# A fused three-block kernel: attention values share the transposes' PSUM bank, dense work gets a third bank, first-batch v tiles are released a third of a step later

## The chip, the cores and the metric

The kernel runs on one core of one Trainium2 chip, in one launch. The metric is the device time of that core in microseconds (us), as a median over runs. One execution was also recorded with the hardware profiler; its trace is what is read below.

## What is computed

Three blocks follow each other. `x` has 4 batches of 576 positions and 512 channels.

```python
# block 1: windowed causal attention, 8 heads of 64, window 128, ALiBi slopes
scores = q @ k.T / 8 ; scores = where(0 <= rel < 128, scores - slope*|rel|, -1e9)
x = softmax(scores) @ v                       # (4, 576, 512)
# block 2: gated unit with a spatial matrix
h = relu(x @ w_in); u, v = h[..., :512], h[..., 512:]
v_n = (v - mean(v)) / sqrt(var(v) + 1e-6)
v_s = w_spatial @ v_n + b_spatial[:, None]
x = (u * v_s) @ w_out                         # (4, 576, 512)
# block 3: four causal attention experts of width 64, the best two of each row mixed
```

Everything is float32. Dense products are made as three TensorE passes over high and low float32r parts (`PASSES`: high by high, high by low, low by high).

## The kernel before, in words

The first phase does blocks 1 and 2 together, the second phase block 3. The change touches the first phase alone.

**Steps.** The first phase walks over 20 query tiles `(b, j)`: 4 batches, 5 tiles of 128 positions each (the last has 64). It is a software pipeline written out by hand: in step `s` the tile `s` gets its scores and its softmax, tile `s-1` gets its probabilities transposed, and tile `s-2` gets its values. TensorE's order is the order of the program text. ScalarE, VectorE and GpSimd are put in order by a compile-time planner that simulates a timeline; each engine then runs its list strictly in that order.

Within one step TensorE's order is this:

- `attend(b, j)` (L416): the values of tile `s-2`, 16 or 32 small matmuls into `px`.
- `scores` (L354, L357): into a two-bank `ps`.
- `take`: ScalarE casts `px` to the high part of `x` (L133), then VectorE subtracts to get the low part (L130, it reads `px` too). Together they release `px`.
- a first pull of dense work, then `parts` (decoding of weights, L219 to L235, in the first steps; later the out weights).
- for each of two groups of heads: `transposes` (L391, 4 or 2 transposes into `pt`), ScalarE's copy of `pt` to SBUF (L392), GpSimd's two triangle selects (L399, L400) on that copy; a pull of dense work; `softmax` (L151, L152) of tile `s`; another pull and `parts`.
- one more pull, so six in a step.

**Dense work.** `Dense` is a queue of generators: for each batch five `v_tile` (L437, 12 matmuls of 512 columns), two `u_half` (L500, four groups of 12 matmuls of 288 columns), one `spatial` (L517 and L522, eight groups of 14). Each pull adds `RATE / 6` = 1367 ns of credit, and passes of the first generator are issued until the credit is used. A generator whose `ready()` is false stops the pull and sets the credit to zero. Each group ends in an evacuation from PSUM: ScalarE Relu for `pv` (L445) and `pu` (L504), VectorE multiply for `pg` (L523). Before the values of tiles `(b, 0)` and `(b, 2)`, `dense.through` issues what is left of the batch before, whatever the credit. Work that follows from a `v` tile (statistics, normalising, the casts `vn`, L448 to L483) is queued in `dense.post`, and every call for dense work emits one piece.

**When a v tile is ready.** `take` writes `xready[b, j] = now[0]`, and a `v_tile` is ready when `now[0]` is larger. `now[0]` is `4 * s` at the start of step `s`, goes up by one after `take`, and by one after each group's `softmax`.

**PSUM.** There are eight banks. `psS` has two buffers of two banks, `psT` one bank (`pt`, and a warm-up tile), `psX` one bank (`px`), `psD` two banks (all dense groups, the decoding of weights, and the fold of two weights after the steps). All of them are closed ahead of the second phase.

Of the kernel before, what the change touches and what calls it, by code (L numbers as in the profile page):

```python
# [9 lines left out]
F32 = mybir.dt.float32  # L10
# [9 lines left out]
PSUM = bass.MemoryType.PSUM  # L20

B, H, S, D = 4, 8, 576, 64
P = 128
# [79 lines left out]
def block_kernel(ctx, tc, qP, kP, v, w_in, wspT, bsp, w_outT, wcat, wo, rel, relt, low, tri, out):  # L103
# [4 lines left out]
    psA = ExitStack()  # L108
    psS = psA.enter_context(tc.tile_pool(name="psS", bufs=2, space=PSUM))
    psT = psA.enter_context(tc.tile_pool(name="psT", bufs=1, space=PSUM))  # L110
    psX = psA.enter_context(tc.tile_pool(name="psX", bufs=1, space=PSUM))
    psD = psA.enter_context(tc.tile_pool(name="psD", bufs=2, space=PSUM))
    dram = ctx.enter_context(tc.tile_pool(name="dram", bufs=1, space=bass.MemoryType.DRAM))

    ident = const.tile([P, P], F32, name="ident")
# [16 lines left out]
    def split(hi, lo, src):  # L132
        nc.scalar.copy(hi, src)  # L133
        lo_part(lo, src, hi)
# [204 lines left out]
    xready, now = {}, [0]  # L339
# [63 lines left out]
    def attend(b, j):  # L403

        q0, qn = TOK[j]
        px = psX.tile([P, 4, P], F32, tag="X", name=f"px{b}_{j}")
        for hp in range(4):
            pT = st_[b, j, hp // 2]
            for t, w in ((j - 1, pT[0]), (j, pT[1])):
                if t < 0:  # L410
                    continue
                kb = TOK[t][1]
                for o in range(2):
                    h = 2 * hp + o
                    rhs = w[:, 2 * (hp % 2) + o, :] if j < 4 else w[:kb, hp % 2, 64 * o : 64 * o + 64]
                    nc.tensor.matmul(px[64 * o : 64 * o + 64, hp, :qn], V_[b, t][:kb, h * 64 : h * 64 + 64], rhs,  # L416
                                     start=(t == max(0, j - 1)), stop=(t == j))
        return px

    def take(b, j, px):  # L420
        q0, qn = TOK[j]
        if j < 4:
            split(x[0][:, :, q0 : q0 + P], x[1][:, :, q0 : q0 + P], px)
        else:
            twice = [t[:, :, 512:640].rearrange("p m (r c) -> p m r c", r=2) for t in x]
            split(*twice, px[:, :, :64].unsqueeze(2).to_broadcast([P, 4, 2, 64]))
        xready[b, j] = now[0]

    stats_, vr = {}, {}

# [155 lines left out]
    low_in(1)  # L586
    add_in(2)
    px = attend(0, 0)
    take(0, 0, px)
    load_in(5)  # L590
    softmax(0, 1, 0)
# [14 lines left out]
    for s in range(2, len(tiles) + 2):  # L606
# [6 lines left out]
        if s > 2:  # L613
            b, j = tiles[s - 2]
            if j in (0, 2) and b > 0:
                dense.through(f"u{b - 1}_{j // 2}")
            px = attend(b, j)
        if s < len(tiles):
            scores(*tiles[s])
        if s > 2:  # L620
            take(*tiles[s - 2], px)
# [109 lines left out]
    psT = ctx.enter_context(tc.tile_pool(name="psTB", bufs=2, space=PSUM, reuse_waits="tile"))  # L731
    psX = ctx.enter_context(tc.tile_pool(name="psXB", bufs=1, space=PSUM, reuse_waits="tile"))
    psD = ctx.enter_context(tc.tile_pool(name="psDB", bufs=3, space=PSUM, reuse_waits="tile"))
# [163 lines left out]
    def attend_b(b, j):  # L897
        qn = TOK[j][1]
        px = psX.tile([P, 4, P], F32, tag="X", name=f"pxB{b}_{j}")
        vt = VS[b]  # L900
        pTs = sb_.pop((b, j))
        for half in range(2):
            for grp, kb, pT in pTs:
                for n, (pr, c, o_) in enumerate(grp):
                    for o in ((o_,) if j < 4 else (0, 1)) if pr == half else ():
                        rhs = pT[:, n, :] if j < 4 else pT[:kb, n, 64 * o : 64 * o + 64]
                        nc.tensor.matmul(px[64 * o : 64 * o + 64, pr, :qn], vt[:kb, c, (2 * pr + o) * 64 : (2 * pr + o) * 64 + 64], rhs,  # L907
                                         start=(c == 0), stop=(c == j))
        return px
# [47 lines left out]
    px = None  # L957
    for s in range(len(tiles) + 2):
        if s < len(tiles):
            b, j = tiles[s]  # L960
# [8 lines left out]
        if s >= 2:  # L969
            px = attend_b(*tiles[s - 2])  # L970
# [91 lines left out]
```

## Time and profile before

| | |
|---|---|
| median of 3 runs | 532.21 us (530.48 to 533.33) |
| profiled execution, its own time | 531.49 us |
| span of its trace | 529.8 us |
| TensorE matmul busy | 496.2 us, 94% of the span |
| VectorE, ScalarE, GpSimd busy | 309.7, 261.3, 98.5 us |
| mean granted TensorE clock | 0.976 of full speed |

The steps run from about 27 us to 285 us of the span, the rest of the dense work and the fold follow, and the second phase takes the rest. The sum in the prediction is made against the profiled execution's own 531.49 us. In the timelines a line is a merged run of like instructions: its start, how long it lasted, engine, line, operation, and in brackets how long the engine sat idle before it and what ended that. Matmul ends are modelled, so starts are better than ends.

### The profile page before, as it was taken

The page shows a single profiled execution, that of the slowest core. Times are in us where ns is not written, and L with a number is a line of the kernel's source. Part 1 is how long each engine was busy: PE and PEld are TensorE (multiplying, and loading weights), DVE is VectorE, ACT ScalarE, POOL GpSimd, SP SyncE. Part 2 cuts the span into 40 slices and gives each one's busy share as a digit, 9 for nine tenths or more (in the row PEclk, how much of TensorE's full clock was granted, in tenths as well). Part 3 has the DMA queues.
Part 4 walks back from the last instruction along what each step waited for, and adds up shares of the span by engine and source line. Part 5 has one row for each costly group of instructions (what it writes and reads, how often), then busy time and mean ns, then how long its engine had stood idle before and what let it go on. Part 6 is the DMA issues. An engine that isn't in the chain of part 4 may idle for free. (4 is left out here: it accounts for less than half of the span.)

```text
span 529.8 us, 10539 instructions
## 1 busy us (share of the span) xinstructions
PE 496.2 (94%) x3910; PEld 430.8 (81%) x3910; DVE 309.7 (58%) x1069; ACT 261.3 (49%) x778; POOL 98.5 (19%) x205
## 2 busy tenths in 40 slices
PE   8879699899996999999999899998989999999995
PEld 6556569798885998799988799997889898897784
DVE  4888777455877566775563622553575564563442
ACT  5655457433655335473353402454564545546552
POOL 0021211212101022102221000103233232231221
PEclk9998979999997999999999899998999999999999
DMA  8921323224231442201204550211000000002331
GB/s 286 361 112 41 97 65 87 104 81 169 81 91 40 152 157 90 69 24 46 104 2 142 192 197 1 91 32 59 1 1 2 2 1 1 1 2 82 124 115 41
DMA packets 25079, 44.34 MB, mean 84 GB/s; under 512 B 5826, under 2 KB 8258, under 8 KB 24644
## 3 DMA queue, kind: packets, MB, share of 16 engines
q1 hardware_dynamic: 24868, 43.54, 24.2%
q8 instruction: 31, 0.51, 0.4%
q10 hardware_dynamic: 160, 0.13, 0.1%
q14 instruction: 20, 0.16, 0.1%
HBM read 32.13 MB, written 11.53 MB: 82 GB/s over the span
## 5 line engine op out<-in xcount | busy, mean ns | idle before, releaser
L152 ACT ACTIVATE p<-p,st 128x128 f32<-128x128 f32 x144 | 56.3, 393 | 46.2 <-DVE st L151 46.2
L437 PE MATMUL pv<-win,x 128*128 128x512 f32 x240 | 64.3, 411 | 3.9 <-ACT x L133 3.7
L500 PE MATMUL pu<-x,win 128*128 128x288 f32 x384 | 58.5, 305 | 7.8 <-ACT u L504 7.8
L517 PE MATMUL pg<-wsp,vn 128*128 128x288 f32 x384 | 61.2, 306 | 2.8 <-ACT u L504 2.8
L500 PEld LDWEIGHTS pu<-x,win 128*128 128x128 f32 x384 | 53.5, 192 | 11.4 <-ACT u L504 9.0
L781 PE MATMUL pq<-x,W 128*128 128x288 f32 x384 | 60.7, 307 | 0.9 <-DVE k L130 0.8
L517 PEld LDWEIGHTS pg<-wsp,vn 128*128 128x128 f32 x384 | 55.0, 195 | 4.3 <-ACT u L504 3.3
L781 PEld LDWEIGHTS pq<-x,W 128*128 128x128 f32 x384 | 53.5, 193 | 4.8 <-issue 2.3
L437 PEld LDWEIGHTS pv<-win,x 128*128 128x128 f32 x240 | 44.1, 193 | 14.4 <-ACT x L133 4.0
L399 POOL TENSOR_SCALAR_AFFINE_SELECT pU<-pT 128x512 f32<-128x512 f32 (+1 forms) x32 | 22.4, 700 | 177.7 <-ACT pT L392 173.6
L159 POOL TENSOR_SCALAR pB<-pB,stB 128x128 f32<-128x128 f32 (+4 forms) x72 | 39.0, 560 | 80.1 <-DVE stB L869 64.8
L152 ACT ACTIVATE pB<-pB,stB 128x128 f32<-128x128 f32 (+3 forms) x64 | 35.6, 558 | 13.6 <-DVE stB L151 13.6
L889 PE MATMUL ptB<-ident,pB 128*128 128x128 f32 (+1 forms) x200 | 31.3, 276 | 3.9 <-POOL pB L159 3.6
L151 DVE CUSTOM_DVE_ANT_0 pB<-psB,trit 128x128 f32<-128x128 f32 (+3 forms) x64 | 28.3, 485 | 11.2 <-PE psB L846 10.5
L805 PE MATMUL pvB<-W,x 128*128 128x260 f32 (+1 forms) x240 | 34.7, 289 | 0.0
L354 PE MATMUL ps<-k,q 64*128 64x256 f32 (+1 forms) x256 | 31.5, 390 | 0.7 <-DMA k<-in_kP 0.7
L805 PEld LDWEIGHTS pvB<-W,x 128*128 128x128 f32 (+1 forms) x240 | 30.1, 178 | 1.1 <-issue 1.1
L928 PE MATMUL pout<-wo,o 128*128 128x512 f32 x108 | 30.1, 409 | 1.0 <-ACT o L133 1.0
L151 DVE CUSTOM_DVE_ANT_0 p<-ps,relm 128x128 f32<-128x128 f32 x128 | 29.6, 286 | 1.5 <-PE pt L391 0.4
L889 PEld LDWEIGHTS ptB<-ident,pB 128*128 128x128 f32 (+1 forms) x200 | 23.7, 139 | 7.6 <-POOL pB L159 4.7
L416 PE MATMUL px<-pT,v 128*64 128x128 f32 (+1 forms) x320 | 28.6, 269 | 1.2 <-POOL pT L400 1.0
L523 DVE TENSOR_TENSOR g<-u,pg 128x288 f32<-128x288 f32 x32 | 14.4, 450 | 25.4 <-PE pg L522 23.2
(147 smaller groups left out, 891.1 us busy)
## 6 DMA issues: line engine op xcount, KB each, us to landing
q<-in_qP SPq DMA_DIRECT2D x20, 256.0 KB, 3.4
g_dram<-g SPq DMA_DIRECT2D x16, 288.0 KB, 2.1
raw<-in_w_in SPq DMA_DIRECT2D x8, 512.0 KB, 6.8
v<-in_v SPq DMA_DIRECT2D x16, 256.0 KB, 3.0
gf<-g_dram SPq DMA_DIRECT2D x4, 1024.0 KB, 5.3
out<-ot SPq DMA_DIRECT2D x16, 256.0 KB, 2.0
k<-in_kP SPq DMA_DIRECT2D x3, 1152.0 KB, 5.4
rawo<-in_w_outT SPq DMA_DIRECT2D x4, 512.0 KB, 4.4
```

The costliest lines, as they stand in the source:

```text
L151: nc.vector.tensor_tensor_reduce(s_view, ps_view, tab, -0.125, FLT_MAX, ALU.add, ALU.min, nm)
L152: nc.scalar.activation(s_view, s_view, AF.Exp, bias=nm, scale=-1.0, accum_out=sm)
L159: nc.gpsimd.tensor_scalar(p, p, r, 0.0, op0=ALU.mult, op1=ALU.add)
L354: nc.tensor.matmul(ps[:, o, 256 * h : 256 * h + kn], Q_[b, j][r, hp, :], K_[b][r, hp, k0 : k0 + kn], start=True, stop=True)
L416: nc.tensor.matmul(px[64 * o : 64 * o + 64, hp, :qn], V_[b, t][:kb, h * 64 : h * 64 + 64], rhs, start=(t == max(0, j - 1)), stop=(t == j))
L437: nc.tensor.matmul(pv, x[i][:, k, t0 : t0 + P], win[j][:, k, 512:1024], start=(n == 0), stop=(n == 11))
L500: nc.tensor.matmul(pu[:, :HALF], win[i][:, k, m * P : (m + 1) * P], x[j][:, k, c], start=(n == 0), stop=(n == 11))
L517: nc.tensor.matmul(pg[:, :HALF], vn[i][k][:, m * P : (m + 1) * P], wsp[j][:, k, c], start=(n == 0), stop=False)
L781: nc.tensor.matmul(pq[:, :HALF], W[i][:, k, c0 : c0 + P], G[j][:, k, c], start=(n == 0), stop=(n == 11))
L805: nc.tensor.matmul(pv[:tn, :260], G[i][:, k, COL[t] : COL[t] + tn], W[j][:, k, 512:772], start=(n == 0), stop=(n == 11))
L889: nc.tensor.transpose(pt[:kb, n, :], p[pr][:, o, c0 : c0 + kb], ident)
L928: nc.tensor.matmul(po[:tn], o2[i][:, pr, :tn], wos[j][:, pr, :], start=(n == 0), stop=(n == 5))
```

## The change

One PSUM pool goes and its bank is given to another. The values tile `px` takes the tag of the transposes' tile in `psT`, so that the transposes of a step wait until `take` has read `px`, and the values of the next step wait until the second group's transposes have been copied out. `psD` gets three banks in place of two. And for batch 0 a `v_tile` becomes ready one count of `now[0]` later: after the first group's `softmax` (the third pull) in place of before the first pull.

```diff
@@ -108,8 +108,7 @@
     psS = psA.enter_context(tc.tile_pool(name="psS", bufs=2, space=PSUM))
     psT = psA.enter_context(tc.tile_pool(name="psT", bufs=1, space=PSUM))
-    psX = psA.enter_context(tc.tile_pool(name="psX", bufs=1, space=PSUM))
-    psD = psA.enter_context(tc.tile_pool(name="psD", bufs=2, space=PSUM))
+    psD = psA.enter_context(tc.tile_pool(name="psD", bufs=3, space=PSUM))
@@ -403,7 +402,7 @@
     def attend(b, j):
-        px = psX.tile([P, 4, P], F32, tag="X", name=f"px{b}_{j}")
+        px = psT.tile([P, 4, P], F32, tag="T", name=f"px{b}_{j}")
@@ -424,7 +423,7 @@
-        xready[b, j] = now[0]
+        xready[b, j] = now[0] + (b == 0)
```

## Rows read from the trace of the kernel before

**Rows 1.** The page, part 1: busy time, share and instructions.

```profile
PE 496.2 (94%) x3910; PEld 430.8 (81%) x3910; DVE 309.7 (58%) x1069; ACT 261.3 (49%) x778; POOL 98.5 (19%) x205
```

**Rows 2.** Who PE waited for, 0 to 330 us: total us, times, longest.

```profile
PE pu L500 <- ACT u L504: 7.8, 5, 4.2
PE pv L437 <- ACT x L133: 3.7, 2, 3.0
PE px L416 <- POOL pU L399: 3.1, 3, 2.0
PE pg L517 <- ACT u L504: 2.8, 2, 2.5
...
PE px L416 <- POOL pT L400: 1.0, 4, 0.3
```

**Rows 3.** Timeline of PE, 74 to 171 us: start us, length us.

```profile
74.29 3.54 PE L354 MATMUL ps<-k,q 64*128 64x256 f32 x16
...
160.42 1.86 PE L500 MATMUL pu<-x,win 128*128 128x288 f32 x12
162.12 0.60 PE L391 MATMUL pt<-ident,p 128*128 128x128 f32 x4
162.47 0.77 PE L500 MATMUL pu<-x,win 128*128 128x288 f32 x4
167.44 3.25 PE L500 MATMUL pu<-x,win 128*128 128x288 f32 x12 [4.20 <-ACT u L504]
```

**Rows 4.** Timeline of all engines, 157 to 171 us, in that same step.

```profile
163.02 0.68 DVE L130 TENSOR_TENSOR x<-px,x 128x512 fp32r<-128x512 f32 x1
...
167.00 0.39 ACT L504 ACTIVATE u<-pu 128x288 f32<-128x288 f32 x1
```

**Rows 5.** Two stretches: length; busy PE, PEld, DVE, ACT, POOL; granted clock; DMA.

```profile
74.30:77.70 3.40, 3.40 (x19) 2.37 (x16) 2.23 (x6) 1.73 (x3) 0.00 (x0) 0.54 0.29 77
...
167.40:170.90 3.50, 3.25 (x12) 2.90 (x12) 2.34 (x11) 2.04 (x9) 1.37 (x2) 0.50 0.00 0
```

**Rows 6.** Timeline of all engines, behind the last step.

```profile
294.02 0.84 ACT L133 CAST wc<-st_wc 128x772 fp32r<-128x772 f32 x1 [2.51 <-DMA st_wc<-in_wcat]
294.76 1.13 ACT L476 CAST vn<-vr 128x512 fp32r<-128x512 f32 x2
...
296.77 3.24 PE L517 MATMUL pg<-wsp,vn 128*128 128x288 f32 x12 [2.52 <-ACT u L504]
```

**Rows 7.** Timeline of all engines, a plain step at 105 us.

```profile
105.52 2.00 PE L354 MATMUL ps<-k,q 64*128 64x256 f32 x16
105.64 0.58 ACT L133 CAST x<-px 128x512 fp32r<-128x512 f32 x1 [3.87 <-PE px L416]
106.26 0.69 DVE L130 TENSOR_TENSOR x<-px,x 128x512 fp32r<-128x512 f32 x1 [2.60 <-ACT x L133]
...
109.42 0.38 PE L391 MATMUL pt<-ident,p 128*128 128x128 f32 x2
```

**Rows 8.** Timeline of all engines, the step at 275 us.

```profile
275.65 0.38 PE L391 MATMUL pt<-ident,p 128*128 128x128 f32 x2
...
277.08 0.68 DVE L130 TENSOR_TENSOR x<-px,x 128x512 fp32r<-128x512 f32 x1
```

**Rows 9.** Timeline of all engines, the first batch at 53 us.

```profile
53.45 2.15 PE L437 MATMUL pv<-win,x 128*128 128x512 f32 x8
...
54.37 0.68 DVE L130 TENSOR_TENSOR x<-px,x 128x512 fp32r<-128x512 f32 x1
```

**Rows 10.** Timeline of all engines, the first batch at 65 us.

```profile
64.67 1.14 ACT L476 CAST vn<-vr 128x512 fp32r<-128x512 f32 x2 [1.22 <-DVE vr L473]
65.72 0.58 ACT L133 CAST x<-px 128x512 fp32r<-128x512 f32 x1
66.34 2.60 PE L437 MATMUL pv<-win,x 128*128 128x512 f32 x8 [3.00 <-ACT x L133]
66.53 0.68 DVE L130 TENSOR_TENSOR x<-px,x 128x512 fp32r<-128x512 f32 x1
```

## The prediction

> **What bounds the kernel now.** I read the page's first part, then TensorE's waits, then the timelines around the longest of them. Matmuls are busy for 496.2 us of the span [rows 1], so TensorE sets the pace and what can be won is the time in which it stands still. In the stretch that the change touches (to 330 us) the list of its waits is short [rows 2]: `pu` for ScalarE's Relu 7.8 us, `pg` for the same 2.8, `pv` for ScalarE's cast of `x` 3.7, and values for GpSimd's selects 3.1 and 1.0. That is 18.4 us, and nearly all of it belongs to something the change alters. Two further things are to be seen. First, ScalarE and VectorE are far from full [rows 1]; they are late because each runs a fixed list in order and a ready evacuation stands behind something that isn't ready. Second, a long stop costs twice: after the 4.20 us stop a group of 12 matmuls takes 3.25 us [rows 3] at a granted clock of 0.50, which is 1.2 in place of 2.4 GHz [rows 5], against 1.86 us for the same group five microseconds earlier [rows 3].
>
> **The third bank for dense work.** The waits of `pu` and `pg` are waits for a bank: TensorE wants to open group n+2 while ScalarE has not read group n. A third bank lets one more group go first. At full clock that is 1.86 us of work for 12 matmuls of 288 columns [rows 3]. Five waits of `pu` make 7.8 us, the longest 4.2, so the other four make 3.6, 0.9 on average and under the 1.86 us of cover; with the small one of `pg` (2.8 less 2.5) I take 3.9 us as gone.
>
> The long wait: the bank comes free when the Relu starts at 167.00 [rows 4], whatever TensorE does. With a third bank the group that now starts at 167.44 and lasts 3.25 us [rows 3] is done before, and TensorE goes on at about 167.4 with the next one. If the clock falls all the same, the gain is the group's work at full clock, 1.86. If the stop is broken into shorter ones and the clock stays up, the 3.25 us are gone, and half of a following group at half clock, about 1.1 (an estimate from 3.25 less 1.86, for eight matmuls in place of twelve, rounded up). So 1.9 to 4.4; I take 3.25, as the stop is broken in two by the transposes (below).
>
> The wait of 2.52 us at 296.77 [rows 6] is also for a bank, but the group needs the casts of `vn` that start at 294.76, held up by a cast that waited for a DMA until 294.02 [rows 6]. The group's fourth matmul needs the first of these two casts, done at about 295.3 (half of 1.13). Starting at 294.25 it loses some 0.5 to 1.5 us on them, so 1.0 to 2.0 of the wait are won, and up to 1.4 more of half clock (3.24 against 1.86). I take 2.0. Sum for the third bank: 3.9 + 3.25 + 2.0 = 9.15, between 6.8 and 12.3.
>
> **The shared bank.** Transposes now wait until VectorE has subtracted from `px`. In a plain step the cast starts at 105.64 and the subtraction ends at 106.95, while the scores run until 107.5 and the transposes come at 109.42 [rows 7]: the scores hide it all, with 2.5 us to spare. It isn't hidden where ScalarE or VectorE come late. At 163.70 the subtraction ends [rows 4], 1.6 us after the transposes at 162.12 [rows 3]; this stop lies inside the one that ends at 167.0 and costs nothing of its own. At 277.76 it ends 2.1 us after the transposes of 275.65 [rows 8]: a loss of 2.1. In the first batch the later v tile takes away the cover: the scores end at 53.45, eight matmuls of `pv` (2.15 us) stood in between, and the subtraction ends at 55.05 [rows 9]: a loss of 1.6. Sum 3.7. It is nought if the planner puts `take` first everywhere; the upper bound is the rival below. The other half of the sharing, values that wait for the copy of the second transposes, is hidden: between them lie two pulls of dense work (2 x 1367 ns of credit), and the selects that the values need wait for this same copy.
>
> The Trainium skill (Perfetto Trace Analysis, Matmuls) says that independent groups should rotate through different banks, so that the reading of one overlaps the next one's matmuls. For dense work the change follows that, for values and transposes it does the opposite. By the rule every step would pay the cast and the subtraction; that is the slower rival below. The plain step does not bear it out, since the scores write elsewhere in the meantime.
>
> **The v tiles of the first batch.** The selects' waits, 3.1 + 1.0 us [rows 2], all stand at the values of the first batch, where nothing lies between the second transposes and the values. With the tile a third of a step later, four matmuls of `pv` lie there, about half of 2.15 us [rows 9]. The longest wait, 2.0, comes ahead of the first tile that moves (tile 0 is ready in step 2 either way), and stays with the 0.3 behind it. The rest, about 1.8, goes.
>
> The 3.00 us at 66.34 [rows 10] are `pv` waiting for the cast of `x`, which stands on ScalarE behind casts of `vn` [rows 10]. After the change the transposes wait in its place, and for the subtraction too, so until 67.21: 0.9 worse, if ScalarE's list stays as it is. But these `vn` follow from v tile 2, which itself ends about a pull later, so I expect the cast of `x` ahead of them; then scores hide all but some 0.3 of cast and subtraction (0.58 + 0.69 from [rows 7] against a start delay and scores that are half as wide here). That wins 2.7, and up to 2.0 of clock: 2.60 against 2.15 us for eight matmuls [rows 9, 10], and 3.54 against 2.00 for the scores at 74.29 [rows 3, 7], which ran at 0.54 [rows 5]. Between -0.9 and 4.7 I take 2.5.
>
> No dense work is lost by the two pulls that now find nothing: what is left of `u0_0` is issued by `dense.through` ahead of the values of (1, 0), as much as now stands before them, and without it 2.7 us of matmuls would only move to the drain at the end. No DMA is added or moved by itself. Sum here: 1.8 + 2.5 = 4.3, between 0.9 and 6.5.
>
> **The sum.** 9.15 - 3.7 + 4.3 = 9.75 us off the profiled execution's 531.49: 521.7. That execution lies 0.7 below the median, so I forecast 522.5. With the ends of each term it is 531.49 - 12.3 - 6.5 = 512.7 at best, and with 6.8, 0.9 and 3.7 a mere 4.0 us, 527.5.
>
> **Rivals.**
> *No change (the wait moves on).* ScalarE is as late as before. Past the third bank TensorE meets the second transposes, which wait for ScalarE's copy of the first, and that copy stands behind the same exponentials as the Relu. Then little more than the small waits go (3.9), the first batch gives its 0.9, and the shared bank takes 3.7: 530.4. For it: all the waits of `pu` have one cause. Against it: the copy is early enough in all other steps.
>
> *Slower (the shared bank becomes the bound).* In each of 19 steps the transposes wait for `take`. If its cast and subtraction, 0.58 + 0.69 = 1.27 us [rows 7], were exposed each time, it costs 24 us against gains of 13.45: 542. It decides from a mean wait of (13.45 + 2.7) / 19 = 0.85 us a step, 2.7 being 0.5% of the time, the least that a measurement of this kernel tells from no change. For it: the planner makes new lists, and one like that at 275.65 costs 2.1. Against it: so far 3.7 us over all steps.
>
> *The v shift wins nothing.* The third bank's 9.15 less the sharing's 3.7 gives 526.
>
> **Chances.** The forecast with all its terms 0.48, the third bank without the shift 0.20, the wait that moves on 0.17, slower 0.15. So faster by over 0.5% 0.68, within 0.5% 0.17, slower 0.15. The range, 515.5 to 533, goes from most of the best terms to past the no-change case; above it lies the slower rival, below it a little. The likeliest case's own range is 515.5 to 527.5.
>
> **What would show it.** Right: `pu <- ACT u` under 3 us in total; no group of `pu` at half clock near 167; a new wait, transposes for VectorE's `x`, of 2 to 5 us in few steps; values waiting for GpSimd at one place only; no wait of `pv` for `x` near 66. Wrong: a wait of the transposes for `x` over 10 us in total, or for the copy `pT` where `pu` waited; a second phase of another length would mean that something outside these steps changed.

## The result, and the profile after

The changed kernel takes 515.34 us (median of four runs, 514.89 to 515.49) against 532.12 (530.48 to 533.33): a ratio of 0.9685, interval 0.9658 to 0.9712, or 16.8 us less. The direction was forecast; the size was not, as the time lies 0.2 us below the range's lower end and 7 us below the forecast. Line numbers after L112 are one less than before, since a line was removed.

The page's first part, after (share of the span and instructions in brackets):

```profile
PE 488.0 (95%) x3910; PEld 425.5 (83%) x3910; DVE 308.4 (60%) x1069; ACT 261.8 (51%) x778; POOL 98.4 (19%) x205
```

The span went from 529.8 to 513.2 us. The same 3910 matmuls are busy for 8.2 us less than in [rows 1]: half of the gain is time in which the same work ran faster, the other half is idle time.

What TensorE waited for, 0 to 330 us, after (total us, times, longest):

```profile
PE pt L390 <- DVE x L129: 6.1, 5, 3.7
PE px L415 <- ACT pT L391: 2.6, 1, 2.6
PE pt L390 <- ACT pT L391: 1.6, 3, 0.7
...
PE pv L436 <- ACT x L132: 0.7, 1, 0.7
```

The waits of `pu` and `pg` of [rows 2], 10.6 us, are gone. The transposes wait for the subtraction of `x` in five places, and the values in one place for the copy of the second transposes.

Where the time went is read from the starts of like instructions in both traces: the first values matmul of tiles (1,0), (2,0), (2,1) and (3,4), the first matmul of the fold (`pw`), and the end. The table (us) has the kernels on which the argument rests; the columns are stages, each from the event before to the one that it names.

| kernel | to (1,0) | to (2,0) | to (2,1) | to (3,4) | to `pw` | to the end |
|---|---|---|---|---|---|---|
| before | 88.02 | 69.44 | 20.87 | 103.64 | 31.16 | 216.63 |
| after | 86.22 | 67.90 | 13.61 | 103.24 | 26.99 | 215.20 |
| e3, sharing alone | 89.37 | 69.58 | 20.44 | 106.96 | 30.16 | 217.13 |
| e1, sharing and third bank | 86.87 | 68.99 | 17.53 | 104.37 | 30.65 | 216.55 |
| e2, later v tiles alone | 89.95 | 67.39 | 14.67 | 102.72 | 27.25 | 216.88 |
| e4, sharing and later v tiles | 86.86 | 68.51 | 14.67 | 104.28 | 27.63 | 215.67 |
| e8, before with 195 ns of credit | 87.34 | 69.78 | 14.66 | 102.73 | 28.78 | 215.31 |
| e9, after without these 195 ns | 86.11 | 67.31 | 16.64 | 104.35 | 30.18 | 218.24 |
| e10, e1 with these 195 ns | 86.67 | 69.03 | 13.61 | 103.25 | 29.91 | 215.18 |
| e5, before with another list at the tail | 86.98 | 69.44 | 20.51 | 103.66 | 26.99 | 216.67 |

Two of the six stages hold 11.4 of the 16.6 us: the one step from (2,0) to (2,1) gave 7.3, and the tail up to `pw` 4.2. The first batch, to which the later v tiles belong, gave 1.8. One profile each is a rough measure of a small difference: e5 has the lists of before in the first batch and still takes 86.98 there against 88.02, so some 1 us of these 1.8 can be two executions of one order.

The same stretches as windows (from and to; length; busy PE, PEld, DVE, ACT, POOL; granted clock; DMA share and GB/s), first of before, then of after:

```profile
157.50:178.30 20.80, 16.37 (x111) 15.01 (x110) 12.04 (x39) 8.66 (x27) 3.68 (x5) 0.84 0.09 34
...
282.00:313.10 31.10, 27.90 (x205) 26.56 (x205) 15.33 (x28) 10.60 (x20) 2.39 (x9) 0.95 0.59 200
313.10:529.70 216.60, 206.63 (x1750) 182.62 (x1748) 104.12 (x380) 106.81 (x292) 49.73 (x118) 0.99 0.11 38
```

```profile
154.10:167.70 13.60, 12.99 (x107) 11.97 (x106) 11.07 (x36) 8.57 (x27) 4.18 (x5) 1.00 0.11 40
...
271.00:298.00 27.00, 26.32 (x206) 25.21 (x206) 14.52 (x28) 10.72 (x20) 2.38 (x9) 1.00 0.70 227
298.00:513.00 215.00, 205.11 (x1749) 181.12 (x1748) 104.02 (x381) 106.80 (x292) 49.74 (x118) 1.00 0.12 39
```

In the step the idle time of TensorE falls from 4.4 to 0.6 us, and the busy time by 3.4, of which four matmuls fewer in the stretch are about 0.6 and the clock, 1.00 in place of 0.84, is the rest. The timeline of after, first that step, then the tail:

```profile
157.07 1.86 PE L499 MATMUL pu<-x,win 128*128 128x288 f32 x12
158.78 0.60 PE L390 MATMUL pt<-ident,p 128*128 128x128 f32 x4
159.13 1.85 PE L499 MATMUL pu<-x,win 128*128 128x288 f32 x12
160.81 1.21 PE L516 MATMUL pg<-wsp,vn 128*128 128x288 f32 x8
162.64 0.66 PE L390 MATMUL pt<-ident,p 128*128 128x128 f32 x4 [0.61 <-ACT pT L391]
...
154.23 0.41 ACT L503 ACTIVATE u<-pu 128x288 f32<-128x288 f32 x1 [0.76 <-PE pu L499]
...
157.92 0.68 DVE L129 TENSOR_TENSOR x<-px,x 128x512 fp32r<-128x512 f32 x1
160.17 0.40 ACT L151 ACTIVATE p<-p,st 128x128 f32<-128x128 f32 x1 [0.32 <-DVE st L150]
161.73 0.39 ACT L503 ACTIVATE u<-pu 128x288 f32<-128x288 f32 x1
...
280.74 1.14 ACT L475 CAST vn<-vr 128x512 fp32r<-128x512 f32 x2 [0.24 <-DVE vr L472]
283.57 0.84 ACT L132 CAST wc<-st_wc 128x772 fp32r<-128x772 f32 x1 [0.86 <-DMA st_wc<-in_wcat]
283.09 1.74 PE L516 MATMUL pg<-wsp,vn 128*128 128x288 f32 x12
```

Three things are to be seen against before. The dense stream stands further ahead: in [rows 3] four matmuls of `pu` followed the transposes and the next group of twelve had to wait, here twelve of `pu` and eight of `pg` follow without one. One Relu stands elsewhere in ScalarE's list: in before the last pass of a group of `pu` is among the matmuls at 160.42 [rows 3], behind the step's scores, and its Relu is the one at 167.00 [rows 4], behind the step's first four exponentials; in after the same group is done ahead of the values of (2,0), and its Relu starts at 154.23, ahead of the exponentials that begin at 160.17. The Relu at 161.73 is that of the next group. And behind the last step the two casts of `vn` stand ahead of the cast of `wc` in ScalarE's list; in [rows 6] they stood behind it and its DMA.

### The profile page after: what moved, and what is told of

The parts are those of the page before. It is cut to its first block, busy times and chain, and to the rows that moved or that the text cites. A ratio compares the mean times of both kernels' runs of the same rounds, so it can differ in the third digit from the quotient of the medians.

```text
span 513.2 us, 10541 instructions
## 1 busy us (share of the span) xinstructions
PE 488.0 (95%) x3910; PEld 425.5 (83%) x3910; DVE 308.4 (60%) x1069; ACT 261.8 (51%) x778; POOL 98.4 (19%) x205
## 5 line engine op out<-in xcount | busy, mean ns | idle before, releaser
L780 PE MATMUL pq<-x,W 128*128 128x288 f32 x384 | 59.4, 303 | 0.9 <-DVE k L129 0.8
L516 PE MATMUL pg<-wsp,vn 128*128 128x288 f32 x384 | 58.9, 298 | 0.1
L780 PEld LDWEIGHTS pq<-x,W 128*128 128x128 f32 x384 | 52.1, 188 | 4.8 <-issue 2.3
L499 PE MATMUL pu<-x,win 128*128 128x288 f32 x384 | 55.1, 298 | 0.0
L516 PEld LDWEIGHTS pg<-wsp,vn 128*128 128x128 f32 x384 | 52.9, 188 | 1.3 <-issue 1.0
L499 PEld LDWEIGHTS pu<-x,win 128*128 128x128 f32 x384 | 52.0, 188 | 1.8 <-issue 0.5
L353 PE MATMUL ps<-k,q 64*128 64x256 f32 (+1 forms) x256 | 29.8, 374 | 0.8 <-DMA k<-in_kP 0.8
L390 PE MATMUL pt<-ident,p 128*128 128x128 f32 x144 | 22.9, 277 | 7.8 <-DVE x L129 6.1
```

Source lines behind the costliest of these rows:

```text
L353: nc.tensor.matmul(ps[:, o, 256 * h : 256 * h + kn], Q_[b, j][r, hp, :], K_[b][r, hp, k0 : k0 + kn], start=True, stop=True)
L499: nc.tensor.matmul(pu[:, :HALF], win[i][:, k, m * P : (m + 1) * P], x[j][:, k, c], start=(n == 0), stop=(n == 11))
L516: nc.tensor.matmul(pg[:, :HALF], vn[i][k][:, m * P : (m + 1) * P], wsp[j][:, k, c], start=(n == 0), stop=False)
L780: nc.tensor.matmul(pq[:, :HALF], W[i][:, k, c0 : c0 + P], G[j][:, k, c], start=(n == 0), stop=(n == 11))
```

## The experiments

Each ratio is to the kernel before on the same chip, with its 95% interval; medians in us. In shares of 532 us, 0.1% is 0.53 us.

**e3: the sharing alone.** Before with `px` in `psT`, and `psX` removed.

```diff
-    psX = psA.enter_context(tc.tile_pool(name="psX", bufs=1, space=PSUM))
-        px = psX.tile([P, 4, P], F32, tag="X", name=f"px{b}_{j}")
+        px = psT.tile([P, 4, P], F32, tag="T", name=f"px{b}_{j}")
```

> Only the shared bank: px lies in the transposes' bank, dense work keeps two banks (one bank stays unused), v tiles are released as before. The instruction order of all engines is the same as in the kernel before, so the difference is the price of the shared bank alone. Theory of the prediction (scores and dense work hide the reading of px in nearly all steps): 2 to 3 us slower, 534 to 535, with transposes waiting for VectorE's x in three or four steps, 2.1 us of it in the step before the last. Rival (every step pays cast and subtraction): 10 us slower or more, 542.

535.37 us, ratio 1.009 (1.0056 to 1.0123): 0.9%, 4.8 us, slower. The order on every engine is that of before, so this is the price of the bank itself. Its largest part, 3.3 us, lies between (2,1) and (3,4), where the transposes wait 2.0 us for `x` at the place that the prediction named near 277.

**e1: sharing and third bank, without the later v tiles.** The changed kernel with the last line undone.

```diff
-        xready[b, j] = now[0] + (b == 0)
+        xready[b, j] = now[0]
```

> Shared bank and third dense bank, without the later v tiles of the first batch. The lists of ScalarE and VectorE are those of the kernel before except behind the last step, where the casts of vn come ahead of a cast that waits for a DMA. Theory that the third bank itself took the waits away: the 4.2 us stop and its half clock go, about 7 us, the small waits 4, the one behind the last step 4, against 2 to 3 for the shared bank: 519 to 521. Rival theory that re-sorted lists did it (through the shift): only the last of these goes, 4 us, less 2 to 3 for the shared bank: 530 to 531.

527.39 us, ratio 0.9946 (0.992 to 0.9972), between the two theories. One clause of the expectation is mistaken: ScalarE's list at the tail is here that of before, as are the orders of all engines throughout. So this run shows what the two changes of banks are worth with no other list. From e3 to e1 the third bank alone gives 1.4%, 7.6 us. It shortens the step at (2,0) by 2.9 us, and the tail not at all (30.16 to 30.65). TensorE's waits in e1:

```profile
PE px L415 <- ACT pT L391: 5.9, 4, 2.6
PE pt L390 <- DVE x L129: 5.5, 4, 2.0
PE pv L436 <- ACT x L132: 3.7, 2, 3.0
PE pg L516 <- ACT u L503: 2.5, 3, 0.9
...
PE pg L521 <- POOL vn L483: 1.1, 1, 1.1
```

Two places in its timeline, the step at (2,0) and the tail:

```profile
162.30 0.66 PE L390 MATMUL pt<-ident,p 128*128 128x128 f32 x4 [1.63 <-DVE x L129]
...
165.99 1.32 PE L516 MATMUL pg<-wsp,vn 128*128 128x288 f32 x8 [0.90 <-ACT u L503]
...
291.01 0.84 ACT L132 CAST wc<-st_wc 128x772 fp32r<-128x772 f32 x1 [2.14 <-DMA st_wc<-in_wcat]
291.76 1.14 ACT L475 CAST vn<-vr 128x512 fp32r<-128x512 f32 x2
292.42 1.49 PE L516 MATMUL pg<-wsp,vn 128*128 128x288 f32 x9 [0.40 <-ACT vn L475]
295.01 0.53 PE L521 MATMUL pg<-wsp,vn 97*128 97x288 f32 x2 [1.10 <-POOL vn L483]
```

With a free bank the long stop of [rows 3] is broken up, as predicted. At the tail the bank is free and TensorE waits for `vn` instead, which stands in ScalarE's list behind the DMA.

**e2: the later v tiles alone.** Before with the last line of the change.

```diff
-        xready[b, j] = now[0]
+        xready[b, j] = now[0] + (b == 0)
```

> Only the later release of the first batch's v tiles; px keeps its own bank and dense work two. The planner sorts ScalarE's and VectorE's lists anew in the steps up to the middle of batch 2. Bank theory: what the trace after shows at the values of (1, 0), 1.8 us, so 529 to 531, and the 4.2 us stop near 162 us is still there. List theory: the evacuations come early enough without a third bank, so the stop goes too: 518 to 522.

520.61 us, ratio 0.9817 (0.9784 to 0.985): 1.8%, 9.7 us faster, with two banks, and although the first batch gets longer (89.95 against 88.02). Where [rows 3] have the stop of 4.20 us, this kernel has, on TensorE:

```profile
160.29 1.86 PE L500 MATMUL pu<-x,win 128*128 128x288 f32 x12
161.99 0.60 PE L391 MATMUL pt<-ident,p 128*128 128x128 f32 x4
162.35 1.84 PE L500 MATMUL pu<-x,win 128*128 128x288 f32 x12
165.40 1.33 PE L517 MATMUL pg<-wsp,vn 128*128 128x288 f32 x8 [1.21 <-ACT u L504]
```

An edit that names only batch 0 removes most of the stop in batch 2, 4.20 us against 1.21. So something is carried there.

**e4: both, with two banks.** The changed kernel with `bufs=2` for `psD`.

```diff
-    psD = psA.enter_context(tc.tile_pool(name="psD", bufs=3, space=PSUM))
+    psD = psA.enter_context(tc.tile_pool(name="psD", bufs=2, space=PSUM))
```

> The change without its third dense bank: shared bank, later v tiles, two dense banks. All lists are those of the changed kernel but for one place. Bank theory: the waits of pu and pg for ScalarE come back, some 8 to 12 us with their half clock, 525 to 529. List theory: hardly any of them come back, 515 to 518.

521.09 us, ratio 0.983 (0.9793 to 0.9867). On top of the later v tiles the sharing costs 0.1% (from e2), no more than the measurement's uncertainty, and the third bank then gives 1.45% (to the changed kernel).

**e8: what is carried is dense credit.** With the later v tiles the first two pulls of step 6, that of the values of (0,4), find nothing, and six passes of batch 0's `u` are left for `dense.through`, which issues them without charging the credit. In the kernel's own bookkeeping the credit ahead of the values of (1,0) is then -53 ns in place of -248. This kernel is before with these 195 ns given at that place, and nothing else:

```diff
+            if (b, j) == (1, 0):
+                dense.credit += 195.0
             px = attend(b, j)
```

> The kernel before with one number added: 195 ns of credit ahead of the values of (1, 0). That is what the later v tiles leave over, since dense.through issues the last passes of u0_0 without charging them. From there on TensorE's order is that of the run with the shift alone; batch 0, the banks and the release of v tiles are as before. Credit theory (the shift won its time because the dense stream runs one pass earlier against the attention steps, so that groups end ahead of a step's exponentials and the planner puts their Relu ahead too): 518 to 521, and the 4.2 us stop is gone. Rival (the later release itself, in batch 0): no change, 530.

521.4 us, ratio 0.9809 (0.9775 to 0.9844): the whole gain of e2, with not one v tile moved. TensorE's order in the two traces shows what the credit does: behind (1,0) the dense work stands one pass, four matmuls, further ahead of the attention work in eleven stretches, one of them the step at (2,0); between them it is level with before, and nowhere behind. TensorE at the same place of this kernel:

```profile
160.07 1.86 PE L500 MATMUL pu<-x,win 128*128 128x288 f32 x12
...
162.13 1.84 PE L500 MATMUL pu<-x,win 128*128 128x288 f32 x12
165.17 1.33 PE L517 MATMUL pg<-wsp,vn 128*128 128x288 f32 x8 [1.20 <-ACT u L504]
```

How this one pass ends the stop is seen in the Relu that moved. In the five kernels of the table with TensorE's order of before at (2,0) (before, e3, e1, and below e9 and e5) the Relu of that group starts 9.2 to 9.7 us after the first values matmul of (2,0); in the five that are one pass ahead (after, e2, e4, e8, and below e10) 0.1 us after it, with two dense banks as with three.

**e9: the changed kernel without these 195 ns.**

```diff
+            if (b, j) == (1, 0):
+                dense.credit -= 195.0
             px = attend(b, j)
```

> The changed kernel with those 195 ns taken off again ahead of the values of (1, 0), so that from there TensorE's order is that of the run with the banks alone; the later v tiles, the shared bank and the third bank stay. Credit theory: 526 to 528, as without the shift. Rival (later release itself): 515 to 517.

522.3 us, ratio 0.983 (0.9792 to 0.9868). Neither number came: about half of what the last line of the change gives beside the banks is the credit, the rest is not. Its timeline has the tail's waits of e1 again, 1.5 us for `vn` on ScalarE and 1.1 for `vn` on GpSimd.

**e10: e1 with these 195 ns.**

```diff
+            if (b, j) == (1, 0):
+                dense.credit += 195.0
             px = attend(b, j)
```

> Shared bank, third bank and the 195 ns of credit, but v tiles released as before. Credit theory: nearly all of the change's gain, 515 to 518. Rival: 527, as with the banks alone.

520.88 us, ratio 0.9799 (0.9761 to 0.9837), again between. With the banks the four kernels make a square: neither 0.9946 (e1), later tiles 0.983 (e9), credit 0.9799 (e10), both 0.9685. The credit is worth 1.45 to 1.47%, the later tiles 1.14 to 1.16%, whichever comes first; by the intervals each of these differences is uncertain by some 0.5%. With the old banks the later tiles add nothing to the credit (e2 and e8). What e10 lacks against the changed kernel is the tail, 29.91 against 26.99, and the later tiles' 1.6 us in the first two stages.

**e5: the order of the lists at the tail alone.** Before with a line at which the planner may move nothing past; TensorE's order stays.

```diff
     dense.through("u3_1")
+    tc.no_sync_barrier()
```

> The kernel before with a fence for the planner behind dense.through of u3_1: TensorE's order is unchanged, and on ScalarE the casts of vn and the Relus of pu come ahead of the cast that waits for a DMA. It leaves two dense banks. Theory that the wait of 2.52 us behind the last step is one of list order: 4 us less (the wait and its half clock), 526. Rival (it needs the third bank): no change, 530.

526.04 us, ratio 0.9894 (0.9862 to 0.9926), as expected. The tail takes 26.99 us, as in the changed kernel, with two banks: 4.2 us less than before. The other 1.4 us by which the profiles differ lie ahead of the edit, where the lists are those of before. All engines at its tail:

```profile
290.36 1.14 ACT L476 CAST vn<-vr 128x512 fp32r<-128x512 f32 x2 [0.23 <-DVE vr L473]
...
292.71 1.74 PE L517 MATMUL pg<-wsp,vn 128*128 128x288 f32 x12
...
293.81 0.84 ACT L133 CAST wc<-st_wc 128x772 fp32r<-128x772 f32 x1 [0.49 <-DMA st_wc<-in_wcat]
```

The casts of `vn` go first and the wait of [rows 6] is gone, the half clock behind it too (1.74 us for the group in place of 3.24). The same order divides the other kernels: where `wc` stands first (before, e3, e1, e9, e10) the tail takes 29.9 to 31.2 us, where `vn` does (after, e2, e4, e8) 27.0 to 28.8, whatever the number of dense banks.

**e11, e12, e13: the two stops that the changed kernel still has in the first batch.** In the changed kernel, at 37.90 and 66.59:

```profile
37.90 0.70 PE L415 MATMUL px<-pU,v 128*64 128x128 f32 x4 [2.55 <-ACT pT L391]
...
41.51 3.18 PE L353 MATMUL ps<-k,q 64*128 64x256 f32 x16
...
63.25 1.66 ACT L475 CAST vn<-vr 128x512 fp32r<-128x512 f32 x3 [1.42 <-DVE vr L472]
64.82 0.58 ACT L132 CAST x<-px 128x512 fp32r<-128x512 f32 x1
...
66.59 0.44 PE L390 MATMUL pt<-ident,p 128*128 128x128 f32 x2 [3.72 <-DVE x L129]
66.78 2.87 PE L436 MATMUL pv<-win,x 128*128 128x512 f32 x8
```

e11 puts a line that nothing is moved past behind `take` of tile (0,3), so that the cast of `x` comes ahead of those of `vn`; e12 holds tile 0's v tile back to stand in front of the values of (0,1); e13 does both.

```diff
             take(*tiles[s - 2], px)
+            if tiles[s - 2] == (0, 3):
+                tc.no_sync_barrier()
```

```diff
     now[0] = 1
+    xready[0, 0] = 9
```

> The changed kernel with a fence for the planner behind take of tile (0, 3): TensorE's order is the same, but ScalarE's cast of x comes ahead of the casts of vn, which is what the prediction had assumed for the change itself. Theory of the prediction for this place: the stop of 3.7 us near 66 and the half clock behind it go, 4 to 5 us less than the changed kernel, 510 to 511.5. Rival (the work that now comes later delays the step's softmax by as much): no change, 515.

> The changed kernel with v tile 0 of batch 0 also a third of a step later, so that four of its matmuls lie between the second transposes of tile 1 and the values of (0, 1). Cover theory: of the 2.55 us stop near 38 about 1.2 us are covered, and the clock may stay up behind it: 1 to 4 us less, 511 to 514. Rival (the stop is set by ScalarE's list, which keeps its order): no change.

> Both edits of the two runs before on the changed kernel. If they are independent, the sum of both gains: 506 to 511.

All three miss: 514.43 us, ratio 0.9703 (0.9657 to 0.9748); 517.23, 0.9737 (0.9705 to 0.9768); 515.75, 0.9712 (0.9676 to 0.9747). None has a lower ratio than the changed kernel's 0.9685. For e11 a small gain isn't excluded: its profile is 1.8 us shorter than that of the changed kernel, with second phases alike (215.17 and 215.20), 0.7 of it by (1,0) and 1.1 by (2,0), but its executions spread from 513 to 519 us. The stops do go, but come back behind. TensorE in e11:

```profile
63.12 0.44 PE L390 MATMUL pt<-ident,p 128*128 128x128 f32 x2 [1.02 <-DVE x L129]
...
69.40 3.65 PE L353 MATMUL ps<-k,q 64*128 64x256 f32 x16
...
77.68 0.66 PE L390 MATMUL pt<-ident,p 128*128 128x128 f32 x4 [2.19 <-ACT pT L391]
```

The stop of 3.72 us is one of 1.02, the values of (0,4) begin 4.2 us earlier (67.30 against 71.54), and at (1,0) 0.7 of it is left: scores at a low clock and a new wait of 2.19 us take the rest. In e12 the decoding of weights waits 2.23 us for VectorE in place of the values.

**e14: one pass more.** The changed kernel with a further 488 ns, one pass, at (1,0).

```diff
+            if (b, j) == (1, 0):
+                dense.credit += 488.0
             px = attend(b, j)
```

> The changed kernel with 488 ns more credit ahead of the values of (1, 0): the dense stream of batches 0 and up runs one pass of four matmuls further ahead. Theory that the place of the groups' ends against the steps decides: the time moves by more than 2 us, either way, with new waits of pt or pu in other steps; with three banks up to 5 us. Rival (only the one lucky place near 162 us mattered, and it is passed already): 514 to 516.

521.28 us, ratio 0.9807 (0.9774 to 0.984). Further ahead is not better: the step at (2,0) takes 12.82 us, the least of all, but the tail 32.93, with its waits for `vn` again, and in ScalarE's list there `wc` stands ahead of `vn`. How far ahead the dense work stands doesn't decide alone; the lists that the planner makes from it count too.

## Why the prediction went wrong

By the ratios, in the order later v tiles (e2), sharing (e4), third bank (the changed kernel): 9.7 us off, 0.7 on, 7.7 off, 16.7 together. Predicted were 4.3 off, 3.7 on, 9.15 off. Of the 7 us that the forecast lacks, the v tiles are 5.4 and the sharing 3.0, and the bank takes 1.4 back.

**The step that failed** is the sentence in the part on the v tiles that no dense work is lost by the two pulls, since `dense.through` issues "as much as now stands before them". That counted matmuls and not credit. Passes that `dense.through` issues are not charged, so 195 ns of credit are left over, and in many later pulls the dense work stands one pass further ahead. The planner then makes other lists for ScalarE and VectorE in places up to the tail. e8 shows that this alone is worth 1.9% without the banks, and e9 and e10 that it is some 1.45% of 3.15% with them. At (2,0) the extra pass lets one group end ahead of the step, and its Relu, which in before stood behind the exponentials, comes at once. How much of the gain there is TensorE's own order and how much the lists the runs don't tell apart, since the credit changes both; for the tail e5 does, it is the lists.

**The v tiles' own terms** were wrong as well. The cast of `x` was to come ahead of those of `vn`; it stayed behind, and the transposes now wait 3.72 us where `pv` waited 3.00 [rows 10]: 0.7 worse, near the lower end that the prediction named, 0.9. The first batch gave 1.8 us in place of 4.3. That the later tiles give a further 1.15% beside the banks (e9) shows in the stages as 0.8 and 1.7 us in the first two and 0.9 at (2,0), against e1. The rest isn't placed: e9's profile took 524.56 us against its median of 522.3, and its second phase, where the program is the same, is 1.7 us longer than e1's.

**The third bank** was sized nearly right, 9.15 predicted against 7.6 and 7.7 by the ratios, but not its pieces; the two pairs of profiles give 8.7 (e3 to e1) and 4.5 (e4 to the changed kernel), so the size is known to a few us only. The upper end of its range, 12.3, doesn't come out of the terms named, which add up to 3.9 + 4.4 + 2.0 + 1.4 = 11.7; the forecast doesn't depend on it. The waits of `pu` go. The 2.0 us at the tail don't belong to it: in e1 a bank is free and the tail is as long as without it, and e5 wins it with two banks. The prediction did see that `vn` stood behind a cast that waited for a DMA [rows 6], but took this order as fixed.

**The shared bank**, 3.7 predicted, costs 4.8 alone and 0.7 with the later v tiles. Of its parts, the values' wait for the copy was called hidden: it is 2.55 us at 37.90, in place of the 2.04 for GpSimd of [rows 2], and clock is lost behind it either way: the scores behind it run at a granted clock of 0.58 in before and 0.62 in after. The 1.6 us expected at 53 [rows 9] were 0.44. The 2.1 us expected at 277 [rows 8] were 2.0 in e3 and 0.9 in the changed kernel, where the lists there are others. The slower rival is refuted by the waits: transposes wait for `x` 6.1 us in five places, not 24 us in 19 steps. The Trainium skill (Perfetto Trace Analysis, Matmuls) says that independent groups should rotate through different banks. The runs agree in both directions: 0.9% is lost where two groups share a bank, and 1.4% is won where dense work gets another. The loss is 4.8 us, not the 24 that it would be if every step paid.

**What was to be seen.** `pu` waiting under 3 us: none is left. No half clock near 167: the step runs at 1.00. Transposes waiting for `x` 2 to 5 us: 6.1, of which 3.72 are the place at 66. No wait of `pv` for `x` near 66: true only because the transposes wait there in its place. Values waiting for GpSimd at one place: at none, for ScalarE's copy at one. The second phase, which the change doesn't touch, is 1.4 us shorter; this goes with the clock, as the last section shows.

## What to carry to other kernels

Where work is metered by credit and an order is planned from it, follow what an edit does to the meter up to the end of the program: here 195 ns at one place were worth 1.5 to 1.9%. Read a wait twice, once for the resource that it names and once for the list in which the releaser stands; a free bank doesn't help an operand that is queued behind a DMA. And an edit in three lines is not three terms: measure each alone and on top of the others before a gain is put down to one of them.

## What the runs showed of the hardware

A stop of about 2 us is followed by a slower stretch in one execution and not in the other. In the second phase the transposes wait 1.92 us for GpSimd in both kernels, and the program there is the same. TensorE in before, then in after:

```profile
360.51 1.52 PE L889 MATMUL ptB<-ident,pB 128*128 128x128 f32 x4 [1.92 <-POOL pB L159]
361.69 4.78 PE L781 MATMUL pq<-x,W 128*128 128x288 f32 x24
```

```profile
345.33 1.37 PE L888 MATMUL ptB<-ident,pB 128*128 128x128 f32 x4 [1.92 <-POOL pB L158]
346.46 3.43 PE L780 MATMUL pq<-x,W 128*128 128x288 f32 x24
```

The 24 matmuls take 4.78 us in the one and 3.43 in the other, 1.35 apart, which is the 1.4 us by which the second phase differs. The granted clock is 0.89 from 355 to 370 us of before, and 1.00 from 340 to 355 of after. Over all fourteen profiles that phase takes 215.2 to 218.6 us, and its length goes with the clock records: 215.2 to 215.7 where the clock stays at 1.00 until the last few us, 216.6 to 217.1 with one stretch at 0.50, 218.2 to 218.6 with two. Why a stop lowers the clock in one execution and not in another stays open. It isn't bound to an edit: executions of the kernel before alone take 528.5 to 534.9 us, at mean clocks of 0.986 to 0.970. For a single profile it means that differences under about 3 us can't be put down to an edit elsewhere.

Half of a gain can be such time: the prediction counted half clock behind single stops [rows 5], and in all 8.2 of the 16.6 us are busy time of the same matmuls, while the mean granted clock rose from 0.976 to 0.988.
